# Values in runs of 17 and sums of one group side by side in PSUM, in a two-layer sliding-window attention kernel

## The chip, the core and the metric

The kernel runs on one core of a Trainium2 chip. The engines are TensorE (PE for its matmuls, PEld for its weight loads), VectorE (DVE), ScalarE (ACT), GpSimd (POOL) and SyncE (SP, which here only issues DMAs). The metric is the device time of one execution in microseconds. Runs of the same kernel agree within some 0.3%.

## What is computed

Two layers over x of 1 x 2048 x 512 in bf16. Each has an attention step with 32 heads of width 16 and a window of 256 keys, and a step that selects one row of the 2048 and adds a gated MLP to it:

```python
def _A_ref(x, wqkv, wo):
    B, S, D = x.shape
    H = 32; Dh = D // H; W = 256
    qkv = (x @ wqkv).reshape(B, S, 3, H, Dh).transpose(2, 0, 3, 1, 4)
    q, k, v = qkv[0], qkv[1], qkv[2]
    scores = jnp.einsum("bhqd,bhkd->bhqk", q, k) * (Dh ** -0.5)
    mask = (idx[:, None] - idx[None, :] >= 0) & (idx[:, None] - idx[None, :] < W)
    scores = jnp.where(mask[None, None], scores, -1e9)
    o = jnp.einsum("bhqk,bhkd->bhqd", _softmax(scores), v)
    return o.transpose(0, 2, 1, 3).reshape(B, S, D) @ wo

x = x + _A_ref(_layernorm(x), A_wqkv, A_wo)
x = x + _B_ref(_layernorm(x), ...)   # one row of 2048 selected, MLP, added
x = x + _A_ref(_layernorm(x), A_wqkv, A_wo)
x = x + _B_ref(_layernorm(x), ...)
```

## The kernel before

The sequence is cut into 16 tiles of 128 rows in each layer, 32 in all. `ln` normalizes a tile, `proj` transposes it (L538), projects q and k (L564) and v (L582), and evicts them with DVE (L571, L573, L590). `kscat` and `vscat` then spread keys and values over partitions with DMAs, into tiles that are block-diagonal over heads.

Scores. 32 heads are 8 groups of 4. For a block of 32 keys, KBD holds the keys of four heads on 64 partitions in such a way that one matmul gives 4 x 32 rows of scores: partition is (head of the group, key), the free axis the query. Two such products, for rows 0 to 63 and 64 to 127 of the array, run as a pair. A *score unit* consists of up to four blocks (L670, eight matmuls) and two matmuls that add the mask (L684); it fills two PSUM banks. There are two such pairs of banks. ACT takes the exponential of a unit into PT (L691).

Values. VBD holds the values for each block of 32 keys: partition 32h + k is key k of the h-th of four heads, and the free axis has two places for heads (only h mod 2 is filled, the other stays zero), so that one product of 64 partitions gives two heads. Each has 17 columns, 16 of values and a column of ones, whose product is the softmax's denominator. The product (L704) has PT as weights, 64 x 128, and 2 x 17 moving columns:

```python
r = e.matmul(acc[:, x, :, 17 * gg:17 * gg + 17], lhsT=self.PT[rows, slot, a, c:c + 128],
             rhs=self.VBD[rows, p3, 4 * tt + b4, :, :, gg], ...)
```

VBD is [128, 3, 8, 2, 17, 8], with the group gg innermost. So `rhs` takes every eighth bf16 element, and `acc` gets two runs of 17 columns, 256 columns apart in the same bank. The two halves x go to the two banks ACC and ACC + 1. A full tile has 12 score units and 192 such matmuls (96 pairs), all of which add into these two banks; there is no second set. After the last one, DVE takes the reciprocal of the denominators (L721) and multiplies (L722) into ON; POOL repeats ON's first 64 columns behind the 512 (L725); `out_proj` transposes ON (L538 again), evicts (L546), multiplies by wo (L741) and adds the residual (L745). The two PSUM banks MISC serve all transposes and projections, one after the other.

Order. All this is recorded as operations with what they read and write, with a PSUM bank set, a priority and an estimated duration (`dur`). `Sched.schedule` then simulates the engines with these estimates: each engine takes, of the operations that are ready by the estimates, the one of lowest priority number. The resulting order per engine is fixed in the program, and semaphore waits are put between engines. A changed `dur` or dependency thus moves instructions on every engine. The estimate of the value products, 50 ns a block and 10 a unit, is the same before and after.

Start. `init` zeroes KBD and VBD on DVE and POOL and writes the ones of VBD (L485); SWC (L495) sums the vector WR16, which a DMA brings.

Of the kernel before, what the change touches and what calls it, by code (L numbers as in the profile page):

```python
# [9 lines left out]
BF16 = mybir.dt.bfloat16  # L10
I32 = mybir.dt.int32
ALU = mybir.AluOpType
# [315 lines left out]
ACC = 4  # L328
MISC = 6
# [7 lines left out]
class Builder:  # L337
# [16 lines left out]
    def alloc(self):  # L354
        nc = self.nc
        NT, SEQ, FF, NF = self.NT, self.SEQ, self.FF, self.NF
# [15 lines left out]
        self.VN = self.sb("VN", [128, 2, 2, 512], BF16)  # L372
        self.VBD = self.sb("VBD", [128, self.RP, 8, 2, 17, 8], BF16)
# [44 lines left out]
        self.VD = nc.dram_tensor("vd", [2, SEQ, 512], BF16)  # L418
# [24 lines left out]
    def init(self):  # L443
        S = self.S
# [3 lines left out]
        for g in range(NT // 2):  # L448
# [7 lines left out]
              writes=["wr16"], nbytes=128 * 1024, name="ld_wr", prio=-6.9)  # L456
# [25 lines left out]
        for p in range(self.RP):  # L482
            S.add("dve", lambda e, p=p: e.memset(self.VBD[:, p].rearrange("p a b c d -> p (a b c d)"), 0.0), writes=["vbz%d" % p], dur=1200, prio=-7.9 + p)
            for h in range(4):
                S.add("dve", lambda e, p=p, h=h: e.memset(self.VBD[32 * h:32 * h + 32, p, :, h % 2, 16, :], 1.0), reads=[],  # L485
                      writes=["vbz%d" % p] + ["vbd%d_%d_%d" % (p, t, h) for t in range(2)], dur=120, prio=-7.8 + p)
# [61 lines left out]
    def proj(self, L, m, at):  # L548
# [39 lines left out]
        vin = self.PS[:, MISC:MISC + 2, :].rearrange("p t (g c) -> p (t g) c", c=128)[:, :, 0:64].rearrange("p g (h d) -> p h d g", d=16)  # L588
        vout = self.VN[:, pr % 2, m % 2].rearrange("p (h d g) -> p h d g", h=4, g=8)
# [23 lines left out]
    def vscat(self, L, m, n, at):  # L613
        S = self.S
        pr = (L * self.NT + m) // 2
        p3, p2, t0 = pr % self.RP, pr % 2, m % 2
        rows = slice(128 * m, 128 * (m + n))
        S.dma("sp", lambda e: e.dma_start(self.VD[L, rows, :].rearrange("(t p) c -> p t c", p=128), self.VN[:, p2, t0:t0 + n, :]),
              reads=["vn%d_%d" % (p2, t) for t in range(t0, t0 + n)], writes=["vd%d_%d" % (L, m)], nbytes=128 * 1024 * n, name="vst", prio=at)
        for h in range(4):  # L620
            def f(e, h=h):
                dst = self.VBD[32 * h:32 * h + 32, p3, 4 * t0:4 * t0 + 4 * n, h % 2, 0:16, :].rearrange("p b d g -> p b (d g)")
                src = self.VD[L, rows, 128 * h:128 * h + 128].rearrange("(b k) c -> k b c", k=32)
                return e.dma_start(dst, src)
            S.dma("sp", f, reads=["vd%d_%d" % (L, m)], writes=["vbd%d_%d_%d" % (p3, t, h) for t in range(t0, t0 + n)], nbytes=32 * 1024 * n, name="vld", prio=at + 0.1)


    def attention(self, L, t, at):
# [5 lines left out]
        acc = self.PS[:, ACC:ACC + 2, :].rearrange("p t (h c) -> p t h c", c=256)  # L634
# [3 lines left out]
        for s in range(4):  # L638
            for u in range(3):
# [55 lines left out]
                def pv(e, blocks=blocks, slot=slot, s=s, u=u):  # L695
                    r = None
                    for (kb, q0, n, c0) in blocks:
                        p3, tt, b4 = loc(kb)
                        c = off_of(u, c0, q0)
                        for a in range(2):  # L700
                            gg = 2 * s + a
                            for x in range(2):
                                rows = slice(64 * x, 64 * x + 64)
                                r = e.matmul(acc[:, x, :, 17 * gg:17 * gg + 17], lhsT=self.PT[rows, slot, a, c:c + 128],  # L704
                                             rhs=self.VBD[rows, p3, 4 * tt + b4, :, :, gg],
                                             start=acc_first[0], stop=(left[0] == 1 and a == 1), skip_group_check=True)
# [12 lines left out]
        accf = self.PS[:, ACC:ACC + 2, :].rearrange("p t (h c) -> p (t h) c", c=256)[:, :, 0:136].rearrange("p h (g c) -> p h g c", c=17)  # L719
        rd = self.RD[:, L, t, :].rearrange("p (h g) -> p h g", g=8)  # L720
        S.add("dve", lambda e: e.reciprocal(out=rd, in_=accf[:, :, :, 16]), banks=[ACC, ACC + 1], writes=["rd%d_%d" % (L, t)], dur=220, name="rden", prio=at)  # L721
        S.add("dve", lambda e: e.tensor_tensor(out=self.ON[:, k2, 0:512].rearrange("p (g h d) -> p h g d", h=4, d=16),  # L722
                                               in0=accf[:, :, :, 0:16], in1=rd.unsqueeze(3).broadcast_to([128, 4, 8, 16]), op=ALU.mult),
              reads=["rd%d_%d" % (L, t)], banks=[ACC, ACC + 1], writes=["on#%d" % k2], dur=600, name="onorm", prio=at)
        S.add("pool", lambda e: e.tensor_copy(out=self.ON[:, k2, 512:576], in_=self.ON[:, k2, 0:64]), reads=[], writes=["on#%d" % k2], dur=150, name="onwrap", prio=at)  # L725

    def out_proj(self, L, t, at):
# [5 lines left out]
        self.transposes(self.ON, k2, ["on#%d" % k2], "tro")  # L733
# [1237 lines left out]
```

## Time and profile before

| | |
|---|---|
| median of 3 runs | 532.86 us (532.82 to 534.0) |
| profiled execution | 531.74 us |
| its span, first to last instruction | 530.0 us |
| mean granted TensorE clock | 0.89 |
| steady tiles | 82 to 265 us (layer 1) and 353 to 478 us (layer 2) |
| start; selection and MLP of layer 1; the same of layer 2 | 0 to 82; 265 to 353; 478 to 530 us |

A row of the page's groups gives the line, engine, operation, output and inputs with their shapes, the count, then the busy time in us, the mean length of one in ns, and the idle time of the engine ahead of them with what ended it. A matmul's shown length contains the time through the array, so that neighbours overlap. In the chain of waits, a row is a start, a length and the work that the end of the program was waiting for at that moment, and lengths of matmuls there go from start to start.

### The profile page before, as it was taken

To read this page: it belongs to the slowest core of one execution; us is meant where nothing else is said; L and a number is where in the kernel's file an instruction comes from. 1 tells how busy PE (TensorE), PEld (TensorE's weight loads), DVE (VectorE), ACT (ScalarE), POOL (GpSimd) and SP (SyncE) were. 2 spreads that over 40 slices of the span, in tenths; PEclk is the share of its full clock that TensorE was granted. 3 is DMA by queue.
4 is the path that set the end of the run, shared out by engine and by line. 5 is a ranking of instruction groups with operands and counts; after the bars stand their busy time and mean duration, and the time that the engine had idled before them with its cause. 6 is when DMAs were issued, how large, how long until landed. Compare 5 with 4: busy or idle time off the path is not lost.

```text
span 530.0 us, 29470 instructions
## 1 busy us (share of the span) xinstructions
PE 448.9 (85%) x13755; PEld 419.2 (79%) x13757; DVE 256.1 (48%) x538; ACT 280.1 (53%) x389; POOL 172.4 (33%) x437
## 2 busy tenths in 40 slices
PE   0358899999999999999997896799999999998971
PEld 0348889998999898999987884798989989897930
DVE  7454445445454444444456407854444444445242
ACT  0014266666666666566664650366566566686600
POOL 8423334322334343332323204733332331213003
PEclk9957899988999998899998758799999889998575
DMA  9971304030313121121313111132222204043000
GB/s 209 378 195 28 62 12 97 4 88 19 83 25 77 30 61 47 52 56 45 63 46 61 34 44 16 47 79 48 74 54 72 56 14 103 14 111 65 5 1 27
DMA packets 104808, 34.46 MB, mean 65 GB/s; under 512 B 87267, under 2 KB 100708, under 8 KB 104421
## 3 DMA queue, kind: packets, MB, share of 16 engines
q1 hardware_dynamic: 97428, 25.07, 20.5%
q10 hardware_dynamic: 7248, 7.41, 4.5%
q8 instruction: 110, 1.80, 1.5%
q14 instruction: 22, 0.17, 0.1%
HBM read 14.30 MB, written 13.96 MB: 53 GB/s over the span
## 4 chain that ended last, share of the span: by engine, by line
PE 76%; DVE 10%; DMA 3%; ACT 3%; ACTq 3%; issue 2%; POOL 1%; DVEq 0%
PE PS L704 34%; PE PS L564 12%; PE PS L670 11%; PE PS L741 7%; PE PS L582 5%; DVE ON L722 3%; ACT PT L691 3%; PE PS L684 3%; PE PS L538 3%; DVE RD L721 2%; DMA WR<-in_B_w_r_dram 2%; PE PS L887 2%; ACTq L439 2%; DMA KBD<-KTN 1%; PE PS L872 1%
## 5 line engine op out<-in xcount | busy, mean ns | idle before, releaser
L691 ACT ACTIVATE PT<-PS 128x768 bf16<-128x768 f32 (+5 forms) x384 | 278.4, 770 | 189.9 <-PE PS L684 184.0
L704 PE MATMUL PS<-VBD,PT 64*128 64x34 bf16 x5760 | 227.8, 237 | 5.6 <-DVE ON L722 4.8
L704 PEld LDWEIGHTS PS<-VBD,PT 64*128 64x128 bf16 x5760 | 190.3, 111 | 9.5 <-DVE ON L722 6.6
L670 PE MATMUL PS<-QT,KBD 64*128 64x128 bf16 (+3 forms) x2880 | 134.5, 214 | 15.4 <-ACT PT L691 10.1
L670 PEld LDWEIGHTS PS<-QT,KBD 64*128 64x128 bf16 x2880 | 97.5, 103 | 23.2 <-ACT PT L691 16.1
L564 PE MATMUL PS<-XNT,WQK 64*128 64x128 bf16 x2048 | 72.6, 233 | 13.1 <-DVE XNT L546 12.9
L684 PE MATMUL PS<-BM,II 64*128 64x64 bf16 (+2 forms) x768 | 81.1, 202 | 0.0
L564 PEld LDWEIGHTS PS<-XNT,WQK 64*128 64x128 bf16 x2048 | 67.5, 104 | 14.2 <-issue 7.2
L523 POOL TENSOR_SCALAR XN<-XR,RS 128x512 bf16<-128x512 bf16 (+1 forms) x32 | 24.5, 765 | 131.2 <-PE PS L538 120.4
L725 POOL COPY ON<-ON 128x64 bf16<-128x64 bf16 x32 | 8.8, 276 | 146.9 <-DVE ON L722 146.9
L745 DVE TENSOR_TENSOR XR<-PS,XR 128x512 f32<-128x512 f32 x32 | 22.1, 692 | 51.6 <-PE PS L741 51.6
L590 DVE CAST VN<-PS 128x512 bf16<-128x512 f32 x32 | 22.1, 692 | 46.1 <-PE PS L582 46.1
L741 PE MATMUL PS<-WO,OT 64*128 64x256 bf16 x512 | 40.6, 307 | 3.9 <-DVE OT L546 3.9
L571 DVE CAST KTN<-PS 128x512 bf16<-128x512 f32 x32 | 22.1, 692 | 44.7 <-PE PS L564 44.6
L684 PEld LDWEIGHTS PS<-BM,II 64*128 64x128 bf16 x768 | 42.4, 101 | 0.0
L546 DVE COPY OT<-PS 128x1024 bf16<-128x1024 bf16 x32 | 22.0, 689 | 31.9 <-PE PS L538 31.9
L582 PE MATMUL PS<-WV,XNT 64*128 64x256 bf16 x512 | 34.4, 274 | 3.3 <-DVE QT L573 1.8
L741 PEld LDWEIGHTS PS<-WO,OT 64*128 64x128 bf16 x512 | 26.7, 106 | 8.9 <-DVE OT L546 4.4
L582 PEld LDWEIGHTS PS<-WV,XNT 64*128 64x128 bf16 x512 | 24.6, 96 | 5.2 <-DVE QT L573 2.0
L538 PE MATMUL PS<-IDB,XN 64*128 64x64 bf16 x512 | 13.9, 196 | 16.8 <-POOL XN L525 13.7
L546 DVE COPY XNT<-PS 128x1024 bf16<-128x1024 bf16 x32 | 22.0, 689 | 9.8 <-PE PS L538 9.7
L538 PEld LDWEIGHTS PS<-IDB,XN 64*128 64x128 bf16 x512 | 11.3, 100 | 18.5 <-POOL XN L525 13.7
(90 smaller groups left out, 357.9 us busy)
## 6 DMA issues: line engine op xcount, KB each, us to landing
scrx<-XR SPq DMA_DIRECT2D x14, 516.0 KB, 3.5
KBD<-KTN SPq DMA_DIRECT2D x120, 32.0 KB, 3.2
vd<-VN SPq DMA_DIRECT2D x15, 256.0 KB, 3.5
VBD<-vd SPq DMA_DIRECT2D x60, 64.0 KB, 3.0
XR<-in_A_x_dram SPq DMA_DIRECT2D x8, 256.0 KB, 8.4
WG<-in_B_w_gate_dram ACTq DMA_DIRECT2D x1, 1792.0 KB, 13.1
WU<-in_B_w_up_dram ACTq DMA_DIRECT2D x1, 1792.0 KB, 17.0
WD<-in_B_w_down_dram ACTq DMA_DIRECT2D x1, 1792.0 KB, 23.4
```

Of the source, the lines that this page charges most:

```text
L523: S.add("pool", lambda e: e.tensor_scalar(out=XN[:, k2, 0:512], in0=x, scalar1=RS[:, k4, 1:2], scalar2=RS[:, k4, 2:3], op0=ALU.mult, op1=A ...
L538: r = e.transpose(o, src[rows, idx, c:c + 128], self.IDB[rows, rows])
L546: S.add("dve", lambda e: e.tensor_copy(out=out, in_=src), banks=[MISC, MISC + 1], writes=[key], dur=620, name=name)
L564: r = e.matmul(self.PS[:, MISC + t, 128 * s:128 * s + 128], lhsT=self.WQK[rows, j, 128 * s:128 * s + 128], rhs=XNT[rows, k2, j, :], start= ...
L571: S.add("dve", lambda e: e.tensor_copy(out=self.KTN[:, pr % 2, m % 2], in_=self.PS[:, MISC + 1, :].rearrange("p (s t) -> p s t", s=4)), ba ...
L582: r = e.matmul(o, lhsT=XNT[rows, k2, j, :], rhs=self.WV[rows, j, :], start=(j == 0), stop=(j == 7))
L590: S.add("dve", lambda e: e.tensor_copy(out=vout, in_=vin), banks=[MISC, MISC + 1], writes=["vn%d_%d" % (pr % 2, m % 2)], dur=600, name="evv")
L670: r = e.matmul(self.PS[:, pair + x, c0:c0 + n], lhsT=self.KBD[rows, p3, tt, s, b4, :], rhs=self.QT[rows, q, s, q0:q0 + n], start=(bi == 0) ...
L684: r = e.matmul(o, lhsT=self.II[rows, :], rhs=w, start=False, stop=True, skip_group_check=True)
L691: return e.activation(out=self.PT[:, slot, :, off:off + ncols], in_=self.PS[:, pair:pair + 2, 0:ncols], func=ACTF.Exp, scale=0.25)
L704: r = e.matmul(acc[:, x, :, 17 * gg:17 * gg + 17], lhsT=self.PT[rows, slot, a, c:c + 128], rhs=self.VBD[rows, p3, 4 * tt + b4, :, :, gg], ...
L741: r = e.matmul(self.PS[:, MISC + x, 0:256], lhsT=self.OT[rows, k2, j, :], rhs=self.WO[rows, j, :], start=(j == 0), stop=(j == 7))
```

## The change

VBD becomes [128, 3, 8, 2, 8, 17]: for each block and head place eight runs of 17, one for each group. The moving operand of L704 is now two runs of 17 elements next to each other in memory, 136 elements apart, and its output is one run of 34 columns of `acc`, so that the sums of one group stand side by side. The ones are no longer written into VBD: VN, the tile into which v is evicted, gets columns of ones once at the start (POOL), the eviction leaves them alone, and the store to VD and the four loads into VBD carry them, 136 columns for each head place instead of 128. VBD is only zeroed at the start. The normalization is split into two instructions, one for each bank, with keys of their own; the estimates of the reciprocal, the two products and POOL's copy are changed to 355, 380 each and 280.

```diff
-        self.VN = self.sb("VN", [128, 2, 2, 512], BF16)
-        self.VBD = self.sb("VBD", [128, self.RP, 8, 2, 17, 8], BF16)
+        self.VN = self.sb("VN", [128, 2, 2, 4, 8, 17], BF16)
+        self.VBD = self.sb("VBD", [128, self.RP, 8, 2, 8, 17], BF16)
...
-        self.VD = nc.dram_tensor("vd", [2, SEQ, 512], BF16)
+        self.VD = nc.dram_tensor("vd", [2, SEQ, 544], BF16)
...
         for p in range(self.RP):
-            S.add("dve", lambda e, p=p: e.memset(self.VBD[:, p].rearrange("p a b c d -> p (a b c d)"), 0.0), writes=["vbz%d" % p], dur=1200, prio=-7.9 + p)
-            for h in range(4):
-                S.add("dve", lambda e, p=p, h=h: e.memset(self.VBD[32 * h:32 * h + 32, p, :, h % 2, 16, :], 1.0), reads=[],
-                      writes=["vbz%d" % p] + ["vbd%d_%d_%d" % (p, t, h) for t in range(2)], dur=120, prio=-7.8 + p)
+            S.add("dve", lambda e, p=p: e.memset(self.VBD[:, p].rearrange("p a b c d -> p (a b c d)"), 0.0), writes=["vbd%d_%d_%d" % (p, t, h) for t in range(2) for h in range(4)], dur=1200, prio=-7.9 + p)
+        S.add("pool", lambda e: e.memset(self.VN[:].rearrange("p a b c d e -> p (a b c d e)"), 1.0), writes=["vn%d_%d" % (a, b) for a in range(2) for b in range(2)], dur=1100, prio=-8.0)
...
-        vin = self.PS[:, MISC:MISC + 2, :].rearrange("p t (g c) -> p (t g) c", c=128)[:, :, 0:64].rearrange("p g (h d) -> p h d g", d=16)
-        vout = self.VN[:, pr % 2, m % 2].rearrange("p (h d g) -> p h d g", h=4, g=8)
+        vin = self.PS[:, MISC:MISC + 2, :].rearrange("p t (g c) -> p (t g) c", c=128)[:, :, 0:64].rearrange("p g (h d) -> p h g d", d=16)
+        vout = self.VN[:, pr % 2, m % 2, :, :, 0:16]
...
-                dst = self.VBD[32 * h:32 * h + 32, p3, 4 * t0:4 * t0 + 4 * n, h % 2, 0:16, :].rearrange("p b d g -> p b (d g)")
-                src = self.VD[L, rows, 128 * h:128 * h + 128].rearrange("(b k) c -> k b c", k=32)
+                dst = self.VBD[32 * h:32 * h + 32, p3, 4 * t0:4 * t0 + 4 * n, h % 2].rearrange("p b g c -> p b (g c)")
+                src = self.VD[L, rows, 136 * h:136 * h + 136].rearrange("(b k) c -> k b c", k=32)
...
-                                r = e.matmul(acc[:, x, :, 17 * gg:17 * gg + 17], lhsT=self.PT[rows, slot, a, c:c + 128],
-                                             rhs=self.VBD[rows, p3, 4 * tt + b4, :, :, gg],
+                                r = e.matmul(acc[:, x, 34 * gg:34 * gg + 34], lhsT=self.PT[rows, slot, a, c:c + 128],
+                                             rhs=self.VBD[rows, p3, 4 * tt + b4, :, gg, :],
...
-        S.add("dve", lambda e: e.reciprocal(out=rd, in_=accf[:, :, :, 16]), banks=[ACC, ACC + 1], writes=["rd%d_%d" % (L, t)], dur=220, name="rden", prio=at)
-        S.add("dve", lambda e: e.tensor_tensor(out=self.ON[:, k2, 0:512].rearrange("p (g h d) -> p h g d", h=4, d=16),
-                                               in0=accf[:, :, :, 0:16], in1=rd.unsqueeze(3).broadcast_to([128, 4, 8, 16]), op=ALU.mult),
-              reads=["rd%d_%d" % (L, t)], banks=[ACC, ACC + 1], writes=["on#%d" % k2], dur=600, name="onorm", prio=at)
-        S.add("pool", lambda e: e.tensor_copy(out=self.ON[:, k2, 512:576], in_=self.ON[:, k2, 0:64]), reads=[], writes=["on#%d" % k2], dur=150, name="onwrap", prio=at)
+        S.add("dve", lambda e: e.reciprocal(out=rd, in_=accf[:, :, :, 16]), banks=[ACC, ACC + 1], writes=["rd%d_%d" % (L, t)], dur=355, name="rden", prio=at)
+        for x in range(2):
+            o = self.ON[:, k2, 0:512].rearrange("p (g x h d) -> p x g h d", x=2, h=2, d=16)[:, x]
+            i0 = accf[:, x].rearrange("p (g h) c -> p g h c", h=2)[:, :, :, 0:16]
+            i1 = rd[:, x, :].rearrange("p (g h) -> p g h", h=2).unsqueeze(3).broadcast_to([128, 8, 2, 16])
+            S.add("dve", lambda e, o=o, i0=i0, i1=i1: e.tensor_tensor(out=o, in0=i0, in1=i1, op=ALU.mult),
+                  reads=["rd%d_%d" % (L, t)], banks=[ACC + x], writes=["on#%d_%d" % (k2, x)], dur=380, name="onorm", prio=at)
+        S.add("pool", lambda e: e.tensor_copy(out=self.ON[:, k2, 512:576], in_=self.ON[:, k2, 0:64]), reads=["on#%d_0" % k2, "on#%d_1" % k2], writes=["on#%d_2" % k2], dur=280, name="onwrap", prio=at)
```

The new kernel's line numbers are one to two off from the old ones (L704 is L702 there, L538 is L536, L582 is L580, L722 is L724). The order moves on all engines. Three places matter to what follows.

PE at the end of the fifth tile, before. The first row is the last group of value products of that tile, the row of 32 belongs to the next tile, and the last row is the transposition of ON, which POOL's copy releases:

```order
L704 MATMUL PS<-VBD,PT 128x2x17 x16
L670 MATMUL PS<-QT,KBD 128x96 x2
L670 MATMUL PS<-QT,KBD 128x128 x4
L670 MATMUL PS<-QT,KBD 128x32 x2
L684 MATMUL PS<-BM,II 128x2x32 x2
L670 MATMUL PS<-QT,KBD 128x32 x2
L670 MATMUL PS<-QT,KBD 128x128 x4
L670 MATMUL PS<-QT,KBD 128x96 x2
L684 MATMUL PS<-BM,II 128x2x32 x2
L704 MATMUL PS<-VBD,PT 128x2x17 x32
L538 MATMUL PS<-IDB,ON 128x64 x16
```

The same place of the changed kernel:

```order
L702 MATMUL PS<-VBD,PT 128x34 x16
L580 MATMUL PS<-WV,XNT 128x4x64 x16
L668 MATMUL PS<-QT,KBD 128x96 x2
L668 MATMUL PS<-QT,KBD 128x128 x4
L668 MATMUL PS<-QT,KBD 128x32 x2
L682 MATMUL PS<-BM,II 128x2x32 x2
L668 MATMUL PS<-QT,KBD 128x32 x2
L668 MATMUL PS<-QT,KBD 128x128 x4
L668 MATMUL PS<-QT,KBD 128x96 x2
L682 MATMUL PS<-BM,II 128x2x32 x2
L702 MATMUL PS<-VBD,PT 128x34 x32
L536 MATMUL PS<-IDB,ON 128x64 x16
```

The projection of v has moved from ahead of the last two groups of value products to behind them; between the last product of a tile and the first of the next there now stand that projection and two score units. In other tiles a third score unit stands there instead.

DVE at the end of the twelfth tile, before:

```order
L721 RECIPROCAL RD<-PS 128x32
L722 TENSOR_TENSOR ON<-PS,RD 128x4x8x16
L546 COPY OT<-PS 128x2x8x64
L745 TENSOR_TENSOR XR<-PS,XR 128x512
L760 BN_STATS ST6M<-XR 128x6
```

And of the changed kernel:

```order
L719 RECIPROCAL RD<-PS 128x32
L724 TENSOR_TENSOR ON<-PS,RD 128x8x32 x2
L544 COPY OT<-PS 128x2x8x64
L746 TENSOR_TENSOR XR<-PS,XR 128x512
L761 BN_STATS ST6M<-XR 128x6
```

Nothing has come between the reciprocal and its products there; the one instruction has become two.

DVE at the start, before. SWC is the sum that waits for the load of WR; XNT is the first transposed tile, for which the first projection waits; the BN rows are layer norms of later tiles:

```order
L514 BN_STATS ST<-XR 128x6 x2
L515 BN_AGGR MV<-ST 128x2 x2
L495 TENSOR_REDUCE SWC<-WR 128x1
L546 COPY XNT<-PS 128x2x8x64
L514 BN_STATS ST<-XR 128x6
L494 CAST IDXV<-IDXI 128x16
```

And of the changed kernel:

```order
L513 BN_AGGR MV<-ST 128x2 x2
L512 BN_STATS ST<-XR 128x6 x2
L493 TENSOR_REDUCE SWC<-WR 128x1
L513 BN_AGGR MV<-ST 128x2 x2
L512 BN_STATS ST<-XR 128x6 x2
L544 COPY XNT<-PS 128x2x8x64
```

Two aggregations and two statistics now stand between SWC and XNT.

For the steady tiles, PE's new order between three successive projections of q and k in layer 1 (the ninth, tenth and eleventh) reads as follows, with S for a score unit, p for a group of 16 value products (p2 for two), V, O for the projections L580 and of wo, X and N for the transpositions of XN and ON. First stretch: S S p2 S p1 V S p1 S S S N S S O p4 X S p1 S p2. Second stretch: S S p2 S V p1 S p1 S p1 S S p1 S N p1 S p2 O S S p2 X S p1 S p1 S.

More of the change, by code (lines that the diff above doesn't have):

```diff
@@ L617, in vscat @@
         rows = slice(128 * m, 128 * (m + n))
-        S.dma("sp", lambda e: e.dma_start(self.VD[L, rows, :].rearrange("(t p) c -> p t c", p=128), self.VN[:, p2, t0:t0 + n, :]),
+        S.dma("sp", lambda e: e.dma_start(self.VD[L, rows, :].rearrange("(t p) c -> p t c", p=128), self.VN[:, p2, t0:t0 + n].rearrange("p t h g c -> p t (h g c)")),
               reads=["vn%d_%d" % (p2, t) for t in range(t0, t0 + n)], writes=["vd%d_%d" % (L, m)], nbytes=128 * 1024 * n, name="vst", prio=at)
@@ L633, in attention @@
         n_units = 12
-        acc = self.PS[:, ACC:ACC + 2, :].rearrange("p t (h c) -> p t h c", c=256)
+        acc = self.PS[:, ACC:ACC + 2, :]
         total = sum(1 for s in range(4) for U in UNITS for b in U if 4 * t + b[0] >= 0)
@@ L718, in attention @@
         S.base = at + 0.9
[L719 to L722, printed above, removed]
-                                               in0=accf[:, :, :, 0:16], in1=rd.unsqueeze(3).broadcast_to([128, 4, 8, 16]), op=ALU.mult),
-              reads=["rd%d_%d" % (L, t)], banks=[ACC, ACC + 1], writes=["on#%d" % k2], dur=600, name="onorm", prio=at)
-        S.add("pool", lambda e: e.tensor_copy(out=self.ON[:, k2, 512:576], in_=self.ON[:, k2, 0:64]), reads=[], writes=["on#%d" % k2], dur=150, name="onwrap", prio=at)
+        accf = self.PS[:, ACC:ACC + 2, 0:272].rearrange("p t (j c) -> p t j c", c=17)
+        rd = self.RD[:, L, t, :].rearrange("p (t j) -> p t j", t=2)
+        S.add("dve", lambda e: e.reciprocal(out=rd, in_=accf[:, :, :, 16]), banks=[ACC, ACC + 1], writes=["rd%d_%d" % (L, t)], dur=355, name="rden", prio=at)
[6 more added lines that the diff above has]
+        S.add("pool", lambda e: e.tensor_copy(out=self.ON[:, k2, 512:576], in_=self.ON[:, k2, 0:64]), reads=["on#%d_0" % k2, "on#%d_1" % k2], writes=["on#%d_2" % k2], dur=280, name="onwrap", prio=at)
     def out_proj(self, L, t, at):
@@ L732, in out_proj @@
         S.base = at
-        self.transposes(self.ON, k2, ["on#%d" % k2], "tro")
+        self.transposes(self.ON, k2, ["on#%d_%d" % (k2, i) for i in range(3)], "tro")
         self.evict_t(self.OT[:, k2], "ot#%d" % k2, "evot")
```

## The prediction

> **What bounds the kernel now.** I read the page first: its span, the engines' busy time, and the chain of waits by line.
>
> ```profile
> span 530.0 us, 29470 instructions
> PE 448.9 (85%) x13755; PEld 419.2 (79%) x13757; DVE 256.1 (48%) x538; ACT 280.1 (53%) x389; POOL 172.4 (33%) x437
> ...
> PE 76%; DVE 10%; DMA 3%; ACT 3%; ACTq 3%; issue 2%; POOL 1%; DVEq 0%
> PE PS L704 34%; PE PS L564 12%; PE PS L670 11%; PE PS L741 7%; PE PS L582 5%; DVE ON L722 3%; ACT PT L691 3%; PE PS L684 3%; PE PS L538 3%; DVE RD L721 2%; DMA WR<-in_B_w_r_dram 2%; PE PS L887 2%; ACTq L439 2%; DMA KBD<-KTN 1%; PE PS L872 1%
> ...
> L691 ACT ACTIVATE PT<-PS 128x768 bf16<-128x768 f32 (+5 forms) x384 | 278.4, 770 | 189.9 <-PE PS L684 184.0
> L704 PE MATMUL PS<-VBD,PT 64*128 64x34 bf16 x5760 | 227.8, 237 | 5.6 <-DVE ON L722 4.8
> ```
>
> PE is nearly always busy and makes 76% of the chain (fourth line); ACT mostly waits for it: 184 us of its idle time end at L684, the last matmul of a score unit. PE's largest group is L704, the 5760 products of probabilities with values. That is the instruction which the change rewrites. Whether its time is on the path, the chain of waits over two steady tiles (224 to 254 us) says:
>
> ```profile
> by line: PE PS L704 44.8%; PE PS L670 12.1%; PE PS L564 11.9%; DVE ON L722 7.0%; PE PS L741 5.8%; PE PS L582 5.8%; PE PS L538 3.7%; DVE RD L721 3.7%; PE PS L684 3.1%; issue 1.4%; POOL ON L725 0.8%
> ...
> 241.67 0.87 PE PS L741 x16
> 242.54 0.50 PE PS L704 x16
> ...
> 243.75 0.17 PE PS L670 x8
> 243.98 0.23 PE PS L538 x16
> ...
> 246.15 1.79 PE PS L564 x64
> ...
> 250.10 0.87 PE PS L582 x16
> ```
>
> Each row is a start, a length and the work. L704 alone makes 44.8% of a steady tile. Now compare two rows of 16 matmuls, each 8 pairs (rows 0 to 63 and 64 to 127 of the array at once) with weights of 64x128: L704 streams 34 columns and takes 0.50 us, 62 ns a pair. L538 streams 64 columns and takes 0.23 us, 29 ns a pair. Half the columns, twice the time: L704 is not held by the streaming of columns, nor by the loading of weights, which L538 has as well.
>
> The granted clock tells more. From 298 to 318 us it was half; the chain of waits and the window rows there:
>
> ```profile
> 301.02 0.48 PE PS L704 x16
> 301.51 0.32 PE PS L670 x8
> ...
> 298.00:318.00 20.00, 18.69 (x497) 16.80 (x498) 3.28 (x14) 11.48 (x16) 0.52 (x2) 0.50 0.13 44
> 224.00:254.00 30.00, 27.85 (x944) 27.01 (x939) 14.17 (x27) 20.63 (x27) 8.74 (x22) 1.00 0.24 52
> ```
>
> The third number from the end of a window row is the clock. At half clock eight score matmuls (L670) go from 0.17 to 0.32 us, nearly as the clock does. L704 stays at 0.48 to 0.50. It is limited by something that doesn't run on TensorE's clock. What sets it apart from all other matmuls here is its moving operand: 34 values that lie 8 elements (16 bytes) apart, and an output in two runs of 17. Both are what the change makes contiguous.
>
> [...]
>
> **The change, part by part.** *L704.* Nothing in the trace reads runs of 17, so I bound it: from above by today's 62 ns a pair (no gain), from below by 15 ns (34 columns at the rate of L564, which streams 128 for each pair in 1.79 us / 32 = 56 ns). The nearest row is L538, with the same weights and 64 columns: 29 ns. I take 30 ns, so 0.24 us for 16 matmuls instead of 0.50. 5760 / 16 = 360 such groups, 360 x 0.26 = 94 us of PE. On the chain of the whole span L704 has 34% of 530 = 180 us, which is 360 x 0.50: nearly all of it lies on the path. (Busy, it shows 227.8 us, since neighbours' modelled ends overlap; the chain's rows go from start to start.)
>
> *What is late next.* A steady tile now, from one reciprocal to the next:
>
> ```profile
> 238.28 0.36 DVE L721 RECIPROCAL RD<-PS 128x32 f32<-128x32 f32 x1 [0.54 <-PE PS L704]
> 238.68 0.69 DVE L722 TENSOR_TENSOR ON<-PS,RD 128x512 bf16<-128x512 f32 x1
> ...
> 248.20 1.52 ACT L691 ACTIVATE PT<-PS 128x768 bf16<-128x768 f32 x2 [1.20 <-PE PS L684]
> 250.13 0.81 ACT L691 ACTIVATE PT<-PS 128x768 bf16<-128x768 f32 x1 [0.41 <-PE PS L684]
> ...
> 252.24 0.36 DVE L721 RECIPROCAL RD<-PS 128x32 f32<-128x32 f32 x1 [0.54 <-PE PS L704]
> ```
>
> It takes 252.24 - 238.28 = 13.96 us. PE's work in it by the rows above: 12 groups of L704 at 0.50, 12 score units at about 0.22 (0.17 and the masks), 1.79, two of 0.87, two of 0.23, together 12.6; the rest is mainly the turnaround at L721 and L722. With 0.24 it is 9.5 us. But ACT has 12 exponentials a tile: 0.75 each in a row (1.52 for two, of which the last shows 0.81), 9.0 to 9.7 us. Two engines of nearly equal load, with only two pairs of score banks between them, don't run without waiting: a score unit must wait for the exponential two units back, and ACT runs dry during L564.
>
> I followed PE's new order by hand through the two stretches between three projections that the part on the change writes out: a score unit 0.22, its exponential 0.44 after its start at the earliest and 0.75 after the one before, the banks free 0.87 after the exponential's start. 11 units took 11.5 us and 14 units 12.6, so 25 units in 24.1: 11.6 us for 12. PE waits for ACT in some 3.5 us of the 24. A tile thus saves 13.96 - 11.6 = 2.4 us of the 3.1 that L704 gives up.
>
> *The split normalization.* L722 becomes two instructions of 256 elements. Rows that bound it: 512 elements take 0.69, and the nearest small ones
>
> ```profile
> L881 DVE TENSOR_TENSOR E<-PS,E 128x14 f32<-128x14 f32 x2 | 0.3, 172 | 0.1
> ```
>
> 14 take 0.17: about 1.04 ns an element and 0.16 fixed, so 0.42 each, 0.85 for both, 0.16 more per tile, at most 32 x 0.16 = 5 us. The new order covers it in part: the value projection (0.87 us) now stands behind the tile's last L704 in some tiles, where before only two score units stood. That is in the 11.6.
>
> *Start.* The zeroing of VBD changes from 1088 words to 2176 halfwords, and POOL fills VN:
>
> ```profile
> L480 POOL MEMSET KBD<- 128x4096 bf16 x1 | 3.5, 3502 | 0.0
> L483 DVE MEMSET VBD<- 128x1088 uint32 x3 | 2.9, 965 | 0.5 <-issue 0.5
> L485 DVE MEMSET VBD<- 32x64 bf16 x12 | 1.2, 112 | 0.4
> ...
> 10.13 9.43 DMA WR<-in_B_w_r_dram
> 19.59 0.69 DVE SWC L495
> ...
> 25.86 0.24 DVE L515 BATCH_NORM_AGGREGATE MV<-ST 128x2 f32<-128x6 f32 x2
> 26.01 1.25 DVE L514 BATCH_NORM_STATS2 ST<-XR 128x6 f32<-128x512 bf16 x2
> ```
>
> At 3502 / 4096 = 0.86 ns an element, 2176 take 1.9 us: 2.8 more on DVE for three, 1.3 less for the twelve small ones, and 1.9 on POOL ahead of the first layer norms. All of it hides behind the load of WR: on the chain of waits DVE stands until 19.59 at L495. Without that cover it would cost some 2 us. Not hidden is what now stands behind L495 and ahead of the copy XNT: two L515 and two L514, 0.24 + 1.25 = 1.5 us on the path.
>
> *At nothing:*
>
> ```profile
> L590 DVE CAST VN<-PS 128x512 bf16<-128x512 f32 x32 | 22.1, 692 | 46.1 <-PE PS L582 46.1
> L571 DVE CAST KTN<-PS 128x512 bf16<-128x512 f32 x32 | 22.1, 692 | 44.7 <-PE PS L564 44.6
> ...
> VBD<-vd SPq DMA_DIRECT2D x60, 64.0 KB, 3.0
> ```
>
> The eviction to VN takes 692 ns with its strided input, as contiguous L571 does: layout doesn't show there. Loads of VBD carry 136 instead of 128 columns, 6% more, about 0.2 us on 3.0; no step of the steady chain waits for them, and behind them in SP's queue stand only other such loads and stores. If that cover went, a tile pair would lose those 0.2 us. The 384 exponentials stay.
>
> **The sum**, stage by stage, from the windows of L704 alone and of everything:
>
> ```profile
> 0.00:82.00 82.00, 15.20 (x384) 12.61 (x384) 0.88 0.55 149
> 82.00:265.00 183.00, 98.24 (x2486) 82.11 (x2488) 0.96 0.23 51
> 265.00:353.00 88.00, 30.70 (x782) 25.57 (x778) 0.81 0.19 42
> 353.00:478.00 125.00, 67.84 (x1732) 56.66 (x1728) 0.96 0.27 63
> 478.00:530.00 52.00, 15.80 (x395) 13.35 (x390) 0.64 0.10 23
> ```
>
> The counts behind the x are matmuls; 16 of them give up at most 0.26 us. 82 to 265: 183 / 13.96 = 13 tiles x 2.4 = 31. 353 to 478: 9 tiles x 2.4 = 21. 0 to 82: at most 24 x 0.26 = 6, half of it to waits for ACT, less the 1.5 of the start: 1.5 left. 265 to 353: at most 49 x 0.26 = 12.7, but much of it is at half clock, where a unit takes 0.32 + 0.05 + 0.48 = 0.85 us and ACT's 0.75 is just beneath: 5. 478 to 530, likewise: 3 of 6.4. Together 61.5 us. The profiled execution took 531.74 us (span 530.0 and 1.7 around it): 531.7 - 61.5 = 470. The median of the runs shown is 1.1 higher, 532.86; I forecast **471 us**.
>
> **Rivals.** *The whole of L704's gain arrives* (13%): waits for ACT stay small, as they are now (3% of the chain), or a pair falls below 29 ns. For it: ACT's floor of 9.0 a tile. 94 us off, less the turnaround and the start: 440 to 446. Against it: two score buffers.
>
> *Only half the gain* (15%): odd runs of 17 that begin at any element are still read slowly, and a pair costs 46 ns, the middle of 62 and 30. For it: no row shows such runs. 16 ns x 2880 pairs = 46 us; by the share that I let through above, 61.5 of 94, 30 of them stay: 503. [...]
>
> *No gain, and slower* (10%): what holds L704 is neither layout but something that stays, its weights from PT or its adding into the same few PSUM columns. For it: L704's weight loads are the longest of their form (111 ns against 96 at L582). Against it: L564 adds into the same columns with every pair, at 56 ns. Then the longer turnaround (at most 5 us) and the start (1.5) remain: 537 to 539. It decides if a pair stays above 60 ns.
>
> ```profile
> L704 PEld LDWEIGHTS PS<-VBD,PT 64*128 64x128 bf16 x5760 | 190.3, 111 | 9.5 <-DVE ON L722 6.6
> L582 PEld LDWEIGHTS PS<-WV,XNT 64*128 64x128 bf16 x512 | 24.6, 96 | 5.2 <-DVE QT L573 2.0
> ```
>
> **How the numbers follow.** The forecast holds 62%, for 455 to 490. The range is 445 to 506: it takes in the half gain and the edge of the full one, and leaves out the slower case and the rest. This kernel's measurement tells 0.3%, 1.6 us, from no change. Faster: 62 + 13 + 15 = 90; same 2, slower 8, both from the last rival.
>
> **What would show it.** In the changed profile, 16 of the value products should take about 0.24 us on the chain, and their length should now differ between full and half clock. A steady tile should take 11.6 us, ACT's exponentials should appear on the chain with over 5%, and the first XNT copy should start near 21.8 us (19.59 + 0.69 + 1.5). I am wrong if the pair stays near 62 ns, if a tile stays above 13 us although it falls (a new wait, first of all for ACT or for ON), or if a PE that idles more is granted less clock than 0.89.

## The result, and the profile after

The changed kernel takes 496.98 us (median of 4 runs, 495.04 to 501.95) against 532.84 us beside it (531.15 to 534.0): ratio 0.934, 95% interval 0.927 to 0.942. Two later sets of runs, each with the kernel before on the same chip, gave 0.949 (0.942 to 0.956) and 0.954 (0.946 to 0.962), that is 505 and 509 us. So the gain is 5 to 7%, some 26 to 36 us of the 61.5 that were forecast. The changed kernel's own runs differ by more than the 0.3% named at the start: by 1.4% in the first set. The profiled execution took 501.95 us, at a mean granted clock of 0.924 where before had 0.89.

The page of the changed kernel: span, engines, the chain of waits by engine and by line, and the groups of the exponentials and of the value products, which are now L702.

```profile
span 500.2 us, 29488 instructions
PE 364.2 (73%) x13757; PEld 319.2 (64%) x13757; DVE 256.5 (51%) x558; ACT 274.4 (55%) x389; POOL 174.6 (35%) x438
...
PE 57%; ACT 13%; issue 11%; DVE 8%; DMA 5%; ACTq 2%; POOL 1%; SPq 0%; DVEq 0%
...
L689 ACT ACTIVATE PT<-PS 128x768 bf16<-128x768 f32 (+5 forms) x384 | 272.6, 772 | 164.7 <-PE PS L682 156.4
...
L702 PE MATMUL PS<-VBD,PT 64*128 64x34 bf16 x5760 | 122.9, 176 | 23.5 <-issue 20.2
L702 PEld LDWEIGHTS PS<-VBD,PT 64*128 64x128 bf16 x5760 | 103.4, 94 | 29.4 <-issue 26.2
```

The products' busy time fell from 227.8 to 122.9 us, even more than forecast, and PE is no longer always busy (73% instead of 85%). Yet the span fell by only 29.8 us. On the chain stand ACT, which was forecast, and "issue" with 11% instead of 2%, which was not: time in which PE waits for nothing that the profile shows. Most of PE's idle time ahead of L702 also ends in "issue".

The same by stage: windows of the changed kernel, cut at the same reciprocals as the stages before, which took 82, 183, 88, 125 and 52 us.

```profile
0.00:77.90 77.90, 42.99 (x1308) 36.84 (x1308) 44.46 (x83) 21.50 (x38) 34.59 (x88) 1.00 0.58 158
77.90:249.20 171.30, 137.15 (x5700) 124.66 (x5701) 87.13 (x181) 116.40 (x158) 63.80 (x161) 0.98 0.25 56
249.20:334.60 85.40, 64.76 (x2074) 53.92 (x2068) 50.40 (x122) 38.31 (x63) 31.51 (x75) 0.80 0.19 47
334.60:449.90 115.30, 90.29 (x3854) 81.62 (x3854) 55.61 (x116) 80.55 (x109) 35.61 (x90) 1.00 0.29 67
449.90:500.20 50.30, 29.02 (x827) 22.14 (x827) 18.86 (x60) 17.62 (x26) 9.04 (x25) 0.65 0.12 28
```

They gained about 4, 12, 3, 10 and 2 us. The 13 steady tiles of layer 1 take 171.3 / 13 = 13.2 us each, not 11.6. That is where the forecast's gain is missing: 22 us in the two steady stages instead of 52.

The chain of waits, by line, for steady tiles (110 to 240 us), first of before, then of the changed kernel:

```profile
by line: PE PS L704 42.7%; PE PS L670 13.1%; PE PS L564 12.4%; PE PS L741 8.5%; PE PS L582 6.1%; DVE ON L722 5.4%; PE PS L538 4.0%; PE PS L684 3.1%; DVE RD L721 2.6%; issue 1.3%; POOL ON L725 0.9%
```

```profile
by line: ACT PT L689 17.7%; PE PS L668 15.7%; PE PS L702 13.7%; issue 13.2%; PE PS L562 13.1%; PE PS L580 7.6%; PE PS L742 6.3%; PE PS L536 4.1%; PE PS L682 2.9%; DVE ON L724 1.2%; POOL XN L521 0.6%; DVE VN L588 0.5%; POOL XN L523 0.5%; DVE
```

Issue is 13.2% of 130 us, 17 us over some ten tiles: 1.7 us a tile. The chain through one tile shows what such a wait looks like:

```profile
354.52 0.40 PE PS L702 x32
354.92 0.27 PE PS L668 x8
355.19 0.06 PE PS L682 x2
355.25 0.06 PE PS L562 x2
355.30 0.89 issue
356.19 1.91 PE PS L562 x62
358.09 0.17 PE PS L668 x8
358.26 0.04 PE PS L682 x2
358.30 0.40 PE PS L702 x32
358.70 0.19 PE PS L668 x8
358.89 0.03 PE PS L682 x2
358.92 0.17 PE PS L702 x14
359.09 0.57 issue
359.66 0.19 PE PS L702 x2
```

PE stops after two of the 64 matmuls of L562, which all have their data, and again before the last two of a group of L702. No wait for data that the profile shows explains such places. But count between the two waits: 62 + 8 + 2 + 32 + 8 + 2 + 14 = 128 matmuls, each with its weight load: 256 instructions. The DMA rows name the supplier:

```profile
q8 instruction: 110, 1.80, 1.5%
```

110 packets, 1.80 MB: 16 KB each, the 27514 instructions of PE in blocks of 256 (27514 / 256 = 107.5). Two of the runs below confirm the block: e4, with 3072 PE instructions fewer (12 x 256), has 98 such packets, and e10, with 2048 more (8 x 256), has 118. In the trace the packets of this queue start 3.8 us apart on average in the steady tiles (4.1 before) and never closer than 3.30 us (3.29 before). A tile has some 860 PE instructions, 3.4 blocks.

The count is no accident of one tile. In the two steady stages of the changed kernel the weight loads stop for over 0.25 us without a wait at 61 places. Of the 59 distances between successive places within a stage, 34 are exactly 128 loads, which with their matmuls are 256 instructions; 15 of the others lie within three loads of 128 or a multiple of it. 57 of the 61 stops end 2.2 to 2.9 us after the start of a packet of that queue. The steady stages of the kernel before have 3 such stops.

**Theory A**: after the change PE outruns the supply of its own instructions. **Rival B**: the tile is set, as the prediction had it, by ScalarE and the work in the array, and "issue" is only where slack shows.

Before, such waits hardly stand on the chain (issue 1.3% of the 130 us, most of it in pieces of 0.02 to 0.14 us around the normalization); after, they do (13.2%).

### The profile page after: what moved, and what is told of

The parts are those of the page before. It is cut to its first block, busy times and chain, and to the rows that moved or that the text cites. A ratio compares the mean times of both kernels' runs of the same rounds, so it can differ in the third digit from the quotient of the medians.

```text
span 500.2 us, 29488 instructions
## 1 busy us (share of the span) xinstructions
PE 364.2 (73%) x13757; PEld 319.2 (64%) x13757; DVE 256.5 (51%) x558; ACT 274.4 (55%) x389; POOL 174.6 (35%) x438
## 4 chain that ended last, share of the span: by engine, by line
PE 57%; ACT 13%; issue 11%; DVE 8%; DMA 5%; ACTq 2%; POOL 1%; SPq 0%; DVEq 0%
ACT PT L689 13%; PE PS L562 12%; PE PS L668 12%; PE PS L702 12%; PE PS L742 6%; PE PS L580 6%; PE PS L536 3%; PE PS L682 2%; PE PS L888 2%; DMA WR<-in_B_w_r_dram 2%; ACTq L439 2%; DMA KBD<-KTN 1%; PE PS L873 1%; DVE VN L588 1%; DVE ON L724 1%
## 5 line engine op out<-in xcount | busy, mean ns | idle before, releaser
L689 ACT ACTIVATE PT<-PS 128x768 bf16<-128x768 f32 (+5 forms) x384 | 272.6, 772 | 164.7 <-PE PS L682 156.4
L668 PE MATMUL PS<-QT,KBD 64*128 64x128 bf16 (+3 forms) x2880 | 130.8, 208 | 41.3 <-ACT PT L689 26.8
L702 PE MATMUL PS<-VBD,PT 64*128 64x34 bf16 x5760 | 122.9, 176 | 23.5 <-issue 20.2
L702 PEld LDWEIGHTS PS<-VBD,PT 64*128 64x128 bf16 x5760 | 103.4, 94 | 29.4 <-issue 26.2
L668 PEld LDWEIGHTS PS<-QT,KBD 64*128 64x128 bf16 x2880 | 84.9, 96 | 57.5 <-ACT PT L689 36.9
L562 PE MATMUL PS<-XNT,WQK 64*128 64x128 bf16 x2048 | 73.7, 232 | 19.1 <-issue 9.8
L562 PEld LDWEIGHTS PS<-XNT,WQK 64*128 64x128 bf16 x2048 | 66.6, 102 | 22.4 <-issue 17.3
L580 PE MATMUL PS<-WV,XNT 64*128 64x256 bf16 x512 | 36.8, 284 | 3.7 <-DVE QT L571 1.7
L742 PE MATMUL PS<-WO,OT 64*128 64x256 bf16 x512 | 35.9, 282 | 3.9 <-DVE OT L544 3.8
L536 PE MATMUL PS<-IDB,XN 64*128 64x64 bf16 x512 | 14.8, 196 | 24.1 <-POOL XN L523 17.2
L580 PEld LDWEIGHTS PS<-WV,XNT 64*128 64x128 bf16 x512 | 25.1, 99 | 7.6 <-DVE QT L571 2.6
L742 PEld LDWEIGHTS PS<-WO,OT 64*128 64x128 bf16 x512 | 24.5, 98 | 7.2 <-DVE OT L544 4.3
L536 PEld LDWEIGHTS PS<-IDB,XN 64*128 64x128 bf16 x512 | 10.4, 98 | 27.9 <-POOL XN L523 17.2
L724 DVE TENSOR_TENSOR ON<-PS,RD 128x256 bf16<-128x256 f32 x64 | 24.3, 418 | 0.8
```

The costliest lines, as they stand in the source:

```text
L536: r = e.transpose(o, src[rows, idx, c:c + 128], self.IDB[rows, rows])
L562: r = e.matmul(self.PS[:, MISC + t, 128 * s:128 * s + 128], lhsT=self.WQK[rows, j, 128 * s:128 * s + 128], rhs=XNT[rows, k2, j, :], start= ...
L580: r = e.matmul(o, lhsT=XNT[rows, k2, j, :], rhs=self.WV[rows, j, :], start=(j == 0), stop=(j == 7))
L668: r = e.matmul(self.PS[:, pair + x, c0:c0 + n], lhsT=self.KBD[rows, p3, tt, s, b4, :], rhs=self.QT[rows, q, s, q0:q0 + n], start=(bi == 0) ...
L689: return e.activation(out=self.PT[:, slot, :, off:off + ncols], in_=self.PS[:, pair:pair + 2, 0:ncols], func=ACTF.Exp, scale=0.25)
L702: r = e.matmul(acc[:, x, 34 * gg:34 * gg + 34], lhsT=self.PT[rows, slot, a, c:c + 128], rhs=self.VBD[rows, p3, 4 * tt + b4, :, gg, :], sta ...
```

## Experiments

### Which side of the product was slow

e1 takes the changed kernel and gives the products the old output again (and the old normalization); e2 takes the kernel before with the new output and normalization.

```diff
 e1: r = e.matmul(
-    acc[:, x, 34 * gg:34 * gg + 34],
+    acc[:, x, :, 17 * gg:17 * gg + 17],
     rhs=self.VBD[rows, p3, 4 * tt + b4, :, gg, :], ...)
 e2: r = e.matmul(
-    acc[:, x, :, 17 * gg:17 * gg + 17],
+    acc[:, x, 34 * gg:34 * gg + 34],
     rhs=self.VBD[rows, p3, 4 * tt + b4, :, :, gg], ...)
```

> Only the moving operand of the value products is contiguous (17 bf16 beside each other); their sums go to PSUM in the old place (two runs of 17, 256 columns apart) and the normalization is the old single one. If the moving operand's 16-byte step was what made a value product slow: 16 of them take about 0.20 us of the chain (0.24 at most), pairs 25 ns apart, time 490 to 505 us as with the whole change. If the two runs in PSUM were: 0.48 to 0.50 us as before, 530 to 540 us.

> The reverse: the values stay 16 bytes apart, and only the sums of a group are 34 contiguous columns of PSUM, with the new split normalization. If the moving operand's step was the cause: 16 value products still take 0.48 to 0.50 us, 530 to 540 us. If the layout in PSUM was: 0.20 to 0.24 us, 490 to 505 us. If both have a part: between, 0.30 to 0.40 us.

e1: 502.9 us (ratio 0.938, 0.929 to 0.947), as fast as the whole change. e2: 527.4 us (0.987, 0.979 to 0.994). The groups of the products in e1, then in e2:

```profile
L702 PE MATMUL PS<-VBD,PT 64*128 64x34 bf16 x5760 | 123.5, 177 | 21.9 <-issue 19.3
```

```profile
L704 PE MATMUL PS<-VBD,PT 64*128 64x34 bf16 x5760 | 226.4, 237 | 3.2 <-issue 1.6
```

The step of 16 bytes in the moving operand makes up all of the difference in L704, and two runs in PSUM cost nothing that shows (123.5 us busy in e1 against 122.9 with one run). e2 is some 8 us faster than before all the same, below the 530 to 540 expected; it is left with the new estimates and the split normalization, which shift the order (which of these brings it wasn't tried apart).

### Less work, the same instructions

e3 halves the columns of the value and output projections.

```diff
-  rhs=self.WV[rows, j, :]
+  rhs=self.WV[rows, j, 0:128]
-  rhs=self.WO[rows, j, :]
+  rhs=self.WO[rows, j, 0:128]
```

> After the change, but the value and output projections multiply only half of their columns (the other half of V and of the output projection is left uncomputed). The number of TensorE instructions is the same, TensorE's work per tile falls by about 0.9 us. Theory A (TensorE now waits for its instructions, 256 of which arrive every 3.4 to 3.8 us): a tile stays at 13.0 us, the time within 5 us of 497, and the waits called issue grow by about what the work falls. Rival B (TensorE's work and ScalarE's exponentials set the tile, as the prediction had it): a tile falls by 0.9 us to 12.1, about 25 us in all, to 470.

With values that are half left over from other products, the kernel's own guard sends it through a second, general path at the end, so the total of 1091.8 us measures nothing. The first pass can be read: the reciprocals, of the changed kernel and of e3, with their count and the first and last start,

```profile
L719 DVE RECIPROCAL RD<-PS x25: 347/349/358, 146.4 to 476.0; 128x32 f32<-128x32 f32 x25
```

```profile
L719 DVE RECIPROCAL RD<-PS x25: 346/357/358, 141.5 to 473.2; 128x32 f32<-128x32 f32 x25
```

The last reciprocal came 2.8 us earlier, not 25, and from the first to the last of the 25 it took 331.7 us instead of 329.6: the tiles are no shorter. The chain of e3 from 110 to 240 us says where the work went:

```profile
by line: ACT PT L689 22.4%; PE PS L668 16.1%; issue 15.8%; PE PS L702 12.8%; PE PS L562 12.6%; PE PS L742 4.3%; PE PS L536 4.2%; PE PS L682 3.1%; PE PS L580 3.0%; DVE ON L724 1.2%; POOL XN L521 0.6%; DVE RD L719 0.6%; DVE OT L544 0.5%; POOL
```

L580 and L742 fell from 13.9 to 7.3% of the 130 us, 8.6 us in some ten tiles; issue and ACT rose from 30.9 to 38.2%, 9.5 us. What PE saves in the array, it waits, so the array's work doesn't set the tile, and that half of rival B falls. But theory A's own sign came only in part: issue rose by 3.4 us, the waits for ACT by 6.1. e3 alone doesn't tell the supply of instructions from ACT.

### Fewer instructions, the same work, and the control

e4 (on the changed kernel) and e9 (on the kernel before) do the projections as matmuls over 128 rows instead of pairs over 64, 3072 instructions fewer, 12 blocks.

```diff
-  for j in range(8):
-      for t in range(2):
-          rows = slice(64 * t, 64 * t + 64)
-          r = e.matmul(self.PS[:, MISC + t, ...], lhsT=self.WQK[rows, j, 128 * s:128 * s + 128],
-                       rhs=XNT[rows, k2, j, :], ...)
+  for j in range(4):
+      for t in range(2):
+          r = e.matmul(self.PS[:, MISC + t, ...], lhsT=self.WQK[:, j, 512 * t + 128 * s:512 * t + 128 * s + 128],
+                       rhs=XNT[:, k2, j, :], ...)
```

> After the change, with the QK, value and output projections as matmuls over 128 rows in place of pairs over 64: half as many instructions for the same work in the array, 96 of about 860 fewer per tile. Theory A: a tile falls by 96 x 14 ns = 1.3 us, 25 to 40 us in all, to 457 to 472, and the waits called issue become fewer. [...]

> The control of run e4: the kernel before with its projections over 128 rows, 3072 TensorE instructions fewer for the same work. Theory A: before waits for instructions in 2% of its chain, so at most 10 us are to be had there, 522 to 536 against e4's 21 us. Rival B'' (matmuls over 128 rows are simply cheaper for TensorE): the same 21 us, 510 to 516.

e4: 476.7 us (0.894, 0.885 to 0.902). e9: 554.8 us (1.044, 1.035 to 1.053). The same edit gains 4 to 6% after the change and loses 4% before it. So it isn't that such matmuls are cheaper; in e9 they are dearer, which neither theory had. The edit also changes how the weights are loaded at the start, so the steady tiles of layer 1 (from the third reciprocal to the sixteenth) are the better measure: 12.2 us in e4 against 13.2 of the changed kernel, 15.3 us in e9 against 14.1 of the kernel before. And issue, 13.2% of the 130 us after the change, is 4.4% in e4:

```profile
by line: ACT PT L684 19.5%; PE PS L663 13.0%; PE PS L558 12.2%; PE PS L697 11.6%; PE PS L736 8.7%; DMA vd<-VN 7.1%; PE PS L575 6.6%; issue 4.4%; DMA VBD<-vd 4.0%; SPq L617 2.8%; PE PS L677 2.3%; PE PS L533 1.7%; DVE XR L740 1.6%; DVE ST6M L
```

The stops for instructions are what the edit removes there. Why such matmuls are dearer, the chain of e9 shows:

```profile
134.74 0.18 PE PS L665 x8
...
134.95 1.89 PE PS L560 x32
136.84 0.28 PE PS L665 x8
...
139.11 0.98 PE PS L577 x8
140.09 0.60 PE PS L699 x16
```

Eight scores (L665, pairs over 64 rows) take 0.18 us, but 0.28 right behind the projection over 128; 16 value products 0.60 instead of 0.50; the projections 1.89 and 0.98 instead of 1.79 and 0.87. Each change between 64 and 128 rows costs 0.1 us, six a tile: at full clock a tile of e9 takes 14.6 us (126.9 to 141.5 us, clock 1.00), 0.6 more than the 13.96 of before. Over 32 tiles that is 19 us, near the 21 that e9 loses, but not the whole account: the clock granted to e9 in the steady tiles of layer 1 was lower too (0.91 instead of 0.96). The changed kernel pays the same. In e4, behind the projection of wo (first row) and around that of v:

```profile
341.86 0.28 PE PS L663 x8
...
348.07 0.98 PE PS L575 x8
349.05 0.30 PE PS L697 x16
```

Eight scores take 0.28 us instead of 0.18, the projection of v 0.98 instead of 0.87, 16 value products 0.30 instead of 0.20. So e4 came out above the 457 to 472 expected. In a steady tile the 96 instructions less (0.375 of a block) brought the 1.0 us that e4 gains and the 0.6 of the changes, some 4.3 us a block. That is more than the 3.8 us between blocks, so a part of it may have another cause; this wasn't taken apart.

### More instructions, the same columns, and the control

e10 (changed kernel) and e11 (before) cut each matmul of the value and output projections in two of 128 columns: 2048 instructions more, 8 blocks. e12 is the changed kernel beside them.

```diff
-  r = e.matmul(self.PS[:, MISC + x, 0:256], lhsT=self.OT[rows, k2, j, :], rhs=self.WO[rows, j, :], ...)
+  for y in range(2):
+      r = e.matmul(self.PS[:, MISC + x, 128 * y:128 * y + 128], lhsT=self.OT[rows, k2, j, :],
+                   rhs=self.WO[rows, j, 128 * y:128 * y + 128], ...)
```

> After the change, with each matmul of the value and output projections cut in two of 128 columns, their weights loaded twice: 2048 TensorE instructions more (8 blocks of 256) for the same columns. Theory A: 7 to 14 ns for each instruction, 14 to 29 us, 511 to 526 at an after of 497. Rival B: TensorE's columns are the same, 0 to 5 us.

> The kernel before with the same cut. Theory A: its blocks come every 4.1 us in the steady tiles and would come every 3.8, still over the 3.3 to 3.4 at which they come at best: 0 to 8 us, 533 to 541. If the second weight load itself costs TensorE time: as much as in e10.

> The changed kernel once more, beside e10, for the difference: 495 to 509.

e12: 505.4 us (0.949). e10: 530.1 us (0.994, 0.989 to 0.999), 24.8 more than e12 and somewhat above the 511 to 526 expected: 3.1 us a block. e11: 542.8 us (1.017, 1.007 to 1.026), 9.3 more, a little above the 0 to 8 expected. As much as these 9.3 us may be the price of the second weight loads in e10 too; then 15.5 us, 1.9 a block, are left for the supply of instructions. Issue in the steady tiles of e12, then of e10, from 110 to 240 us:

```profile
by line: ACT PT L689 18.9%; PE PS L668 15.1%; issue 14.5%; PE PS L702 13.2%; PE PS L562 13.1%; PE PS L580 7.0%; PE PS L742 6.3%; PE PS L536 3.9%; PE PS L682 2.8%; DVE ON L724 1.2%; POOL XN L521 0.6%; DVE VN L588 0.5%; POOL XN L523 0.5%; DVE
```

```profile
by line: issue 19.3%; ACT PT L691 15.2%; PE PS L562 14.1%; PE PS L670 13.9%; PE PS L704 13.7%; PE PS L745 7.6%; PE PS L581 6.7%; PE PS L536 3.3%; PE PS L684 2.7%; DVE ON L726 1.8%; DVE VN L590 1.1%; DVE RD L721 0.7%
```

In e11 it is 1.8%. Of a steady tile of layer 1 (13.2 us in e12, 14.4 in e10, 14.6 in e11) issue is 1.9 us in e12 and 2.8 in e10, but 0.2 in before and 0.3 in e11. The added instructions show as issue after the change; before it they do not.

### No-operations: inconclusive

> After the change, with 8 no-operations on TensorE between the two mask products of each of the 384 score units: 3072 instructions more, 12 blocks of 256, nothing more to compute. Theory A: where instructions come 256 in 3.4 to 3.8 us, 12 blocks are 41 to 46 us; at least 30 us of it shows, 527 to 545. Rival B (a no-operation costs only the time it takes to step over it, with or without the change): as much as in the kernel before with the same no-operations, the run beside this one.

> The kernel before with the same 3072 no-operations. Its TensorE takes a block of 256 in 4.2 us on average of the steady tiles, 0.5 to 0.8 us longer than the blocks need, so theory A gives a part of what run e5 loses: 5 to 20 us, 537 to 555. Rival B: the same loss as in e5.

```diff
+  if x == 1:
+      for _ in range(8):
+          e.nop()
   r = e.matmul(o, lhsT=self.II[rows, :], rhs=w, ...)
```

509.2 us (0.954) and 534.7 us (1.000, 0.996 to 1.004). Both profiles still show 13757 + 13757 PE instructions and 110 instruction packets: the no-operations are not in the program that ran, and the 527 to 545 and 537 to 555 expected of them could not come. e5 is thus one more set of runs of the changed kernel, and tells nothing between the theories.

### How far it goes

e7 adds to e4 transposes of 128x128 (4 instead of 16); e8 adds to e7 the value products over 128 rows, with VBD block-diagonal over four heads.

```diff
 e7:
-  for j in range(8):
-      for t in range(2):
-          r = e.transpose(o, src[rows, idx, c:c + 128], self.IDB[rows, rows])
+  for j in range(4):
+      r = e.transpose(self.PS[:, MISC, :].bitcast(BF16)[:, 128 * j:128 * j + 128], src[:, idx, 128 * j:128 * j + 128], self.IDB[:])
 e8:
-  for x in range(2):
-      r = e.matmul(acc[:, x, 34 * gg:34 * gg + 34], lhsT=self.PT[rows, slot, a, c:c + 128], rhs=self.VBD[rows, p3, 4 * tt + b4, :, gg, :], ...)
+  r = e.matmul(acc[:, gg // 4, 68 * (gg % 4):68 * (gg % 4) + 68], lhsT=self.PT[:, slot, a, c:c + 128], rhs=self.VBD[:, p3, 4 * tt + b4, :, gg, :], ...)
```

> Run e4 with the transposes as 4 of 128x128 in place of 16 of 64x128, and without the 64 wrapped columns that these needed: 1536 TensorE instructions fewer (22906 of 24442) and two small GpSimd copies per tile less. Theory A: e4 fell by 21 us for 3072 fewer, 6.8 ns each, so another 5 to 12 us, 465 to 472 at a before of 533. Rival B': the instruction supply is no longer the limit behind e4 (its waits called issue are 6% of the chain), the tile is now set by ScalarE and TensorE's work: 0 to 3 us, 474 to 477.

> Run e7 with the value products too over 128 rows: one matmul with 68 columns (four heads in one block-diagonal, half of it zeros) in place of a pair with 34, 17146 TensorE instructions; four buffers of exponentials in place of five to make room. Theory A: waits called issue nearly gone (under 2% of the chain), tiles 10.5 to 11.5 us where ScalarE is busy 9: 430 to 455. Rival B': the 68 columns cost as much as the pair saves, and nothing is won against e7: 465 to 477.

e7: 460.8 us (0.859, 0.850 to 0.867), 16 less than e4, more than the 5 to 12 expected, and the fastest of all: it beats both kernels. It also leaves out two small POOL copies a tile, so the 16 us are not the instructions' alone. e8, which has the normalization in one instruction besides and four buffers of exponentials instead of five: 475.2 us (0.887, 0.880 to 0.894), a miss of theory A's 430 to 455 and within rival B' (465 to 477). Its chain:

```profile
379.52 0.98 PE PS L571 x8
380.50 0.26 PE PS L691 x8
380.76 0.28 PE PS L659 x8
381.04 0.06 PE PS L673 x2
381.09 0.38 PE PS L691 x8
```

Issue is 2% of e8's chain and its steady tiles of layer 1 take 12.7 us each, so the supply is no longer felt. But scores (L659) and products (L691) now alternate between 64 and 128 rows: 0.28 instead of 0.18 and 0.38 instead of 0.26 at each change. And eight products over 128 rows take 0.26 us, 32 ns each, against 25 ns for a pair. Two changes in each of 12 units, 0.1 us each, are 2.4 us a tile, more than the 1.7 us that the waits called issue had cost a tile of the changed kernel.

## Why the prediction was right or wrong

*Direction, and L704: right, and undersized.* The layout was the limit, and by e1 and e2 the moving operand alone. 16 products take 0.20 us instead of the 0.24 taken from L538 (between the bounds of 15 and 62 ns a pair: 25), so single matmuls start 12.5 ns apart. That the length should now differ between full and half clock came true, but by little. Around the fall of the clock, in the changed kernel:

```profile
277.13 0.20 PE PS L702 x16
...
284.68 0.45 PE PS L702 x32
...
285.51 0.45 PE PS L702 x30
```

and the window row there, whose third number from the end is the clock:

```profile
277.50:287.00 9.50, 6.83 (x266) 6.31 (x264) 2.52 (x13) 7.15 (x11) 1.59 (x4) 0.50 0.13 40
```

The first is from just before the clock fell, 12.5 ns a matmul; the other two, at half clock, 14 and 15 ns. In the whole trace a pair takes 25 ns at full clock and 29 at half (medians), so the product doesn't follow the clock as the scores do (0.17 to 0.32 us for eight).

*What is late next: the step that failed.* "PE waits for ACT in some 3.5 us of the 24", and 11.6 us a tile. ACT's waits came as forecast in kind (17.7% of the chain, where 3.5 us of 24 are 15%). But the step knew only two limits, the array and ACT. A third, the supply of PE's instructions, was put at nothing and takes 1.7 us a tile, about what the tile is longer than forecast (13.2 instead of 11.6 us). Before stood close to it (a block every 4.1 us on average, 3.3 at the least), but hardly a stop showed it there: it could be read from the starts of the instruction packets alone. The sign named for being wrong, a tile above 13 us, came; the guess at its cause, ACT or ON, did not.

*The split normalization:* 0.42 us each forecast,

```profile
L724 DVE TENSOR_TENSOR ON<-PS,RD 128x256 bf16<-128x256 f32 x64 | 24.3, 418 | 0.8
```

is right; the 5 us it might cost are not seen (e1, without the split, is no faster, and e2, with it, is faster than before).

*Start:* XNT forecast at 21.8 us:

```profile
20.43 0.69 DVE L493 TENSOR_REDUCE SWC<-WR 128x1 f32<-128x512 bf16 x1 [4.49 <-DMA WR<-in_B_w_r_dram]
21.04 0.24 DVE L513 BATCH_NORM_AGGREGATE MV<-ST 128x2 f32<-128x6 f32 x2
21.19 1.25 DVE L512 BATCH_NORM_STATS2 ST<-XR 128x6 f32<-128x512 bf16 x2
...
22.36 0.67 DVE L544 COPY XNT<-PS 128x1024 bf16<-128x1024 bf16 x1
```

It came 2.1 us later than before (20.27) instead of 1.5. The four instructions behind SWC took 1.2 us, about as forecast; the rest is SWC itself, 0.8 later, since the load of WR ended later. The stage to 82 us still gained 4 us where 1.5 was forecast; what gained there is not shown.

*At nothing:* the eviction to VN takes 693 ns (692 before), as forecast; the loads of VBD land in 2.5 us (3.0), sooner, where 0.2 us more was allowed for.

*The sum* failed by the tiles alone: 22 us in the steady stages instead of 52, and the rest 8 where 9.5 was forecast. The range held the first result by luck: its upper end of 506 was drawn to take in a value product at half the gain, and the product gained more than forecast (0.30 us for 16, not 0.26), while another term brought the time there. The sets of 505 and 509 us lie at its upper edge and beyond.

*Clock.* The worry that an idling PE is granted less clock didn't come true here: busy 73% of the span instead of 85%, it was granted 0.924 instead of 0.89, in the steady tiles of layer 1 0.98 instead of 0.96.

Open remain why a block takes 3.3 us at the least, and why the blocks come 3.8 us apart on average when 3.4 of them at 3.3 us would fill only some 11 us of the 13.2 of a tile: no run tells how the stops and the waits for ACT depend on each other, makes ACT faster, adds score banks or takes other transfers out of the way of the instruction packets. Open is also why the same kernel came out between 497 and 509 us in three sets while the kernel before stayed at 533 to 535; the granted clock doesn't settle it (0.927 at 496.26 us, 0.928 at 504.67).

## What to carry to other kernels

When the matmuls of a dense, unrolled kernel become short, count instructions, not only columns: here, in the steady tiles, PE got 256 of them, 128 matmuls with their loads, in no less than 3.3 us, and waits called "issue" in the middle of a group, 256 instructions apart at 34 of 59 distances, were the sign. Then one matmul over 128 rows can be worth more than two over 64: it was in e4, with six changes between the two forms a tile (12.2 us a tile instead of 13.2), and not in e8, with two more in every score unit (475.2 us against e7's 460.8). And the step of a moving operand can cost more than the matmul itself: 37 ns a pair here, on top of 25.

## What was not expected of the hardware

- The supply of PE's instructions: in the steady tiles blocks of 256 start at least 3.3 us apart, 13 ns an instruction; eight more blocks for the same columns cost 24.8 us after the change and 9.3 before it.
- Each change between matmuls over 64 and over 128 rows costs 0.1 us at full clock (eight scores 0.28 us instead of 0.18), in e9 0.6 us a tile.
- 34 moving columns at a step of 16 bytes cost 62 ns a pair, contiguous 25; the layout of the output in PSUM (34 together, or two runs of 17) makes no difference that shows (122.9 and 123.5 us busy).
